# First block of a fused layernorm, state-space and mish kernel: one vector multiply placed behind the last rotation, the next x loaded two phases earlier, its layernorm pieces one to three first-layer tiles earlier

## The chip, the cores and the metric

The kernel runs on one core of one Trainium2 chip. The metric is device time in microseconds (us) of one execution, by default as the median of several. The profile's own span is about 2 us shorter than the device time of the same execution (623.9 against 626.0 for the kernel before), so spans are compared only with spans, and times with times.

Names used below: PE is the TensorE matmul engine, DVE is VectorE, ACT is ScalarE, POOL is GpSimd, SP is SyncE, which here only issues transfers. A bank is one of the eight pieces `ps[:, bank, :]` (512 fp32 values per partition) into which the kernel divides PSUM, the memory that its matmuls write to.

## The reference, cut to what matters

The input x is 2048 rows of 1024. After a layernorm the same rows feed two branches, which are added to x:

```python
xn = layernorm(x)
# branch A: complex diagonal recurrence over the 2048 rows
Bu = xn @ B_bar.T                      # 1024 complex states
h_t = Lam_bar * h_{t-1} + Bu_t
y  = 2 * real(h @ C.T) + xn * Dskip
# branch B: dense, mish, dense
h  = xn @ w1 + b1                      # 3584 wide
act = h * tanh(log1p(exp(h)))          # mish, written stably
out = x + y + act @ w2
```

The kernel works in four blocks of 512 rows. In each block PE does the first dense layer (28 tiles, f=0 to 27, eight matmuls each), the input projection of the recurrence (j=0 to 7, 16 matmuls each), then the second dense layer and the output projection, called the tail below.

## The kernel before: the parts that the change and the argument touch

The kernel issues each engine's work in the order of the source, and in its timelines each engine's operations run in that order. A helper works out the semaphore waits from the buffers that an operation reads and writes, so moving a line of source moves the operation in its engine's queue, and nothing else.

The end of the first layer and the side work of the first block (cut to block 0):

```python
def first_tile(blk, f):                 # PE: 8 matmuls into bank f % 8
    ...
    if fi == 1:
        item_done()                     # two tiles used up: SP may load the slot anew
    if f % GF == 0 and f >= 2 * GF:
        mish_mul(f // GF - 2)           # DVE: multiplies 0 and 1, at f = 14 and 21
    vop(... hb[:, hs, :] = ps[:, bank, :] + b1(f))       # DVE: frees the bank (L648)
    if f % GF == GF - 1:
        mish(f // GF)                   # ACT: exp, ln, tanh of seven tiles

def side(f):                            # block 0
    ...
    if f in (9, 11, 12, 13):  ln_skip(0, ...)
    if f in (14, 16, 18, 20): ln_stats_only(1, ...)      # statistics of the next x
    if f == 22:               ln_rsqrt()                 # 15 operations on 4 columns
    if f in (23, 24, 25, 26): ln_scale(1, ...)
    if f < 16 and f % 2 == 0: transpose_B(f // 2)        # SP: two transposing transfers
    if f >= 16:               transpose_C(f - 16)
```

POOL computes the phases of the rotation tables and issues the next x among them:

```python
for j in range(NJ):
    phases(j)                           # POOL: px, py, and the difference of both
    if j == 3:
        for q in range(NQ):
            load_x(PO, 1, q)            # four transfers of 256 KB
```

The input projection, with the rotation of its result on DVE (the "rotation" of j below means these four operations):

```python
def project_in(blk):
    for j in range(NJ):
        bank = 2 * ((j + 2) % 4)        # banks 4-5, 6-7, 0-1, 2-3, and again
        ... 16 matmuls into bank and bank + 1 (L661)
        for s in range(2):
            vop(... mt[:, s] = u * tab[:, s, j])          # L666, reads PSUM
        vop(... hT[:, 0, j] = mt[0, 0] + mt[1, 1])        # L669
        vop(... hT[:, 1, j] = mt[0, 1] - mt[1, 0])        # L671
        if j == (6 if blk == 0 else 4):
            mish_mul(2)                 # DVE, 128 x 3584 (L626)
        if j == 7 and blk:
            mish_mul(3)
```

The tail (L715) begins with 24 matmuls into banks 4 to 7; the next ones go to banks 0 to 3:

```python
for f in range(6):
    dense(f, ..., (4, 5, 6, 7))
for f in range(NF):
    dense(f, ..., (0, 1, 2, 3) if f < 6 else range(8))
```

## Time and profile before

Before the prediction the kernel had been timed three times: 625.97, 626.24 and 626.64 us.

| Kernel before | |
|---|---|
| median time | 626.24 us |
| span of the profiled execution | 623.9 us |
| PE busy / DVE busy / ACT busy | 99% / 75% / 40% |
| start of one 128x512 matmul to the next, undisturbed | 0.216 us |
| PE waits after its start-up | one, of 1.5 us |

The first line is the profile page's table of busy time per engine.

```profile
PE 616.7 (99%) x2961; PEld 287.4 (46%) x2961; DVE 466.0 (75%) x695; ACT 247.1 (40%) x162; POOL 50.0 (8%) x47
```

PE is the limit. The question for a small change is therefore only where PE stands still. The PE timeline of the kernel before (start, length, operation, count; a bracket tells the idle time just before the group and what ended it) shows one such place after the start-up:

```profile
83.80 3.62 PE L661 MATMUL ps<-xnT,BT 128*128 128x512 bf16 x16
87.25 5.78 PE L715 MATMUL ps<-ring,act 128*128 128x512 bf16 x26
94.55 5.79 PE L715 MATMUL ps<-ring,act 128*128 128x512 bf16 x26 [1.52 <-DVE mt L666]
```

The tail starts at 87.25 us, does its 24 matmuls and two more, and then waits. The bracket says 1.52 us, measured from the modelled end of the last matmul, which overlaps the next one when nothing waits. The real loss is counted from start to start: 26 matmuls at 0.216 us after 87.25 is 92.87 us, and the next one started at 94.55, so 1.68 us were lost.

The DVE timeline of the same stretch shows what was waited for:

```profile
67.45 2.34 DVE L666 TENSOR_TENSOR mt<-ps,tab 128x1024 bf16<-128x1024 f32 x2
...
87.14 2.36 DVE L666 TENSOR_TENSOR mt<-ps,tab 128x1024 bf16<-128x1024 f32 x2
...
90.21 2.02 DVE L626 TENSOR_TENSOR act<-act,hb 128x3584 bf16<-128x3584 bf16 x1
92.14 2.35 DVE L666 TENSOR_TENSOR mt<-ps,tab 128x1024 bf16<-128x1024 f32 x2
...
95.20 2.34 DVE L681 TENSOR_TENSOR_SCAN hT<-cs,hT 128x512 bf16<-128x512 f32 x2
```

The eight rotations start at 67.45 us and follow each other without a pause. The multiply of 1.93 us stands between j=6 and j=7. The products of j=7, which free banks 2 and 3, end at 92.14 + 2.35, so at 94.5 us, and PE starts then.

### The profile page before, as it was taken

The numbers are of one execution on the slowest core, as the hardware profiler recorded it, in microseconds if no ns is written. First come the engines' busy times: TensorE is split into PE (matmuls) and PEld (weight loads), VectorE is DVE, ScalarE is ACT, GpSimd is POOL, SyncE is SP. The second block draws the span as 40 slices with busy tenths as digits, with TensorE's granted clock in tenths as the row PEclk, the third lists the DMA queues.
The fourth block names the chain that finished last, engine by engine and source line by source line (L and its number), as shares of the span: only waits on it lengthen the run. The fifth ranks groups of instructions, "written<-read, shape, count | busy, mean of one in ns | idle before, by whom it ended". The sixth has DMA issues, their size and how long they took to land.

```text
span 623.9 us, 7415 instructions
## 1 busy us (share of the span) xinstructions
PE 616.7 (99%) x2961; PEld 287.4 (46%) x2961; DVE 466.0 (75%) x695; ACT 247.1 (40%) x162; POOL 50.0 (8%) x47
## 2 busy tenths in 40 slices
PE   8999999999999999999999999999999999999998
PEld 7644444444444444444444444444444444444443
DVE  6799999999457599999047759999624856999603
ACT  6679995441059950000008992000001999000000
POOL 1899000000100000000010000000000000000000
PEclk9999999999999999999999999999999999999999
DMA  9999976750365400764065520285204532033001
GB/s 268 215 259 249 258 152 172 200 166 3 106 198 169 134 2 7 232 171 132 13 190 144 159 101 1 77 227 153 85 35 134 167 137 68 1 131 106 1 0 68
DMA packets 124188, 79.41 MB, mean 127 GB/s; under 512 B 48890, under 2 KB 106490, under 8 KB 124154
## 3 DMA queue, kind: packets, MB, share of 16 engines
q1 hardware_dynamic: 120656, 71.58, 42.9%
q10 hardware_dynamic: 2538, 4.21, 1.8%
q0 software_dynamic: 960, 3.15, 1.8%
q8 instruction: 24, 0.39, 0.3%
q14 instruction: 10, 0.08, 0.0%
HBM read 63.19 MB, written 4.19 MB: 108 GB/s over the span
## 4 chain that ended last, share of the span: by engine, by line
PE 95%; DVE 3%; DMA 1%; issue 0%; SPq 0%; DVEq 0%
PE ps L715 48%; PE ps L641 29%; PE ps L661 16%; DVE mt L666 2%; PE ps L499 2%; DMA xx<-in_A_x_dram 1%; DVE hT L669 0%; PE ps L383 0%; DVE hT L671 0%; DVE xn L376 0%; SPq L287 0%; DVE xnT L392 0%; DVE xx L752 0%; DVE rs L371 0%; DVE stats L341 0%
## 5 line engine op out<-in xcount | busy, mean ns | idle before, releaser
L715 PE MATMUL ps<-ring,act 128*128 128x512 bf16 x896 | 194.2, 379 | 1.5 <-DVE mt L666 1.5
L641 PE MATMUL ps<-xnT,ring 128*128 128x512 bf16 x848 | 183.7, 379 | 0.0
L619 ACT ACTIVATE act<-hb 128x3584 bf16<-128x3584 bf16 x16 | 50.9, 3183 | 246.2 <-DVE hb L648 245.9
L715 PEld LDWEIGHTS ps<-ring,act 128*128 128x128 bf16 x896 | 87.5, 98 | 107.6 <-DVE mt L666 2.0
L641 PEld LDWEIGHTS ps<-xnT,ring 128*128 128x128 bf16 x848 | 82.9, 98 | 99.9
L648 DVE TENSOR_SCALAR hb<-ps,par 128x512 bf16<-128x512 f32 x112 | 82.8, 747 | 55.3 <-PE ps L641 54.0
L661 PE MATMUL ps<-xnT,BT 128*128 128x512 bf16 x512 | 111.2, 379 | 0.0
L715 PE MATMUL ps<-CT,hT 128*128 128x512 bf16 x512 | 111.2, 379 | 0.0
L666 DVE TENSOR_TENSOR mt<-ps,tab 128x1024 bf16<-128x1024 f32 x64 | 75.4, 1219 | 13.2 <-PE ps L661 11.7
L661 PEld LDWEIGHTS ps<-xnT,BT 128*128 128x128 bf16 x512 | 50.0, 98 | 60.5
L715 PEld LDWEIGHTS ps<-CT,hT 128*128 128x128 bf16 x512 | 50.0, 98 | 60.5
L752 DVE TENSOR_TENSOR xx<-ps,xx 128x1024 bf16<-128x1024 f32 (+1 forms) x17 | 19.5, 1161 | 72.0 <-PE ps L715 72.0
L681 DVE TENSOR_TENSOR_SCAN hT<-cs,qi,hT 128x512 bf16<-128x512 f32 x48 | 58.9, 1269 | 0.0
L621 ACT ACTIVATE act<-act 128x3584 bf16<-128x3584 bf16 x16 | 51.0, 3190 | 0.2
L620 ACT ACTIVATE act<-act 128x3584 bf16<-128x3584 bf16 x16 | 51.0, 3190 | 0.2
L686 DVE TENSOR_TENSOR mt<-hT,tab 128x1024 bf16<-128x1024 bf16 x64 | 41.4, 688 | 1.1
L626 DVE TENSOR_TENSOR act<-act,hb 128x3584 bf16<-128x3584 bf16 x16 | 32.3, 2017 | 1.3 <-ACT act L621 1.3
L287 POOL DMA_DIRECT2D xx<-in_A_x_dram x12 | 6.7, 559 | 254.8 <-DVE xx L752 250.5
L595 ACT ACTIVATE ct<-CT,cs 128x512 f32<-128x512 bf16 x16 | 11.5, 718 | 29.1 <-DVE CT L597 24.5
L620 ACT ACT_TABLE_LOAD x16 | 20.5, 1283 | 0.3
L621 ACT ACT_TABLE_LOAD x16 | 20.5, 1283 | 0.3
L681 DVE TENSOR_TENSOR_SCAN hT<-cs,hT 128x512 bf16<-128x512 f32 x16 | 18.7, 1208 | 0.0
(82 smaller groups left out, 280.2 us busy)
## 6 DMA issues: line engine op xcount, KB each, us to landing
ring<-in_B_w_dram SPq DMA_DIRECT2D x112, 512.0 KB, 3.7
out_dram<-xx ACTq DMA_DIRECT2D x15, 256.0 KB, 2.0
xx<-in_A_x_dram POOLq DMA_DIRECT2D x12, 256.0 KB, 4.0
xx<-in_A_x_dram SPq DMA_DIRECT2D x4, 256.0 KB, 3.4
dsk<-in_A_Dskip_dram SPq DMA_DIRECT2D x1, 256.0 KB, 6.4
out_dram<-xx ACTq DMA_DIRECT2D x2, 128.0 KB, 1.7
xnT<-xn SPq DMA_TRANSPOSE x12, 4.5
BT<-in_A_B_re_dram SPq DMA_TRANSPOSE x8, 5.9
```

The source lines that it names most:

```text
L619: aop(lambda e: e.activation(a, hs, AF.Exp), reads=[b_hb[g % 2]], writes=[b_act[g]])
L620: aop(lambda e: e.activation(a, a, AF.Ln, bias=1.0), reads=[b_act[g]], writes=[b_act[g]])
L621: aop(lambda e: e.activation(a, a, AF.Tanh), reads=[b_act[g]], writes=[b_act[g]])
L626: vop(lambda e: e.tensor_tensor(a, a, hs, op=ALU.mult), reads=[b_act[g], b_hb[g % 2]], writes=[b_act[g]])
L641: PE.mm(lambda e, k=k: e.matmul(ps[:, bank, :], lhsT=wt[:, k, fi * P:(fi + 1) * P], rhs=xnT[:, k, :], start=k == 0, stop=k == NK - 1), rea ...
L648: vop(lambda e: e.tensor_scalar(hb[:, hs, :], ps[:, bank, :], b1(f), None, op0=ALU.add), reads=[b_ps[bank], b_par], writes=[b_hbf[hs]])
L661: PE.mm(lambda e, j=j, ci=ci, k=k, bank=bank: e.matmul(ps[:, bank + ci, :], lhsT=BT[:, ci, j, k, :], rhs=xnT[:, k, :], start=k == 0, stop= ...
L666: vop(lambda e, s=s, u=u, j=j: e.tensor_tensor(mt[:, s, :, :], u, tab[:, s, j, :].unsqueeze(1).to_broadcast([P, 2, TB]), op=ALU.mult), rea ...
L681: vop(lambda e, ci=ci, init=init: e.tensor_tensor_scan(out=hT[:, ci, j, :], data0=cj("r", j).to_broadcast([P, TB]), data1=hT[:, ci, j, :], ...
L686: vop(lambda e, s=s: e.tensor_tensor(mt[:, s, :, :], hT[:, :, j, :], tab[:, s, j, :].unsqueeze(1).to_broadcast([P, 2, TB]), op=ALU.mult), ...
L715: PE.mm(lambda e: e.matmul(ps[:, u, :], lhsT=lhsT, rhs=rhs, start=st_, stop=last), reads=reads, writes=[b_ps[u]], first=st_, last=last)
L752: vop(lambda e: e.tensor_tensor(xr, src, xr, op=ALU.add), reads=b_src + [b_x], writes=[b_x])
```

## The change

The intent is to let j=7 free its banks before the multiply runs, and to spread the remaining DVE work of the first block so that the rotations start no later. The x of the second block has to arrive earlier for that. The whole diff:

```diff
     for j in range(NJ):
         phases(j)
-        if j == 3:
+        if j == 1:
             for q in range(NQ):
                 load_x(PO, 1, q)
@@ project_in
-            if j == (6 if blk == 0 else 4):
+            if j == 4 and blk:
                 mish_mul(2)
-            if j == 7 and blk:
-                mish_mul(3)
+            if j == 7:
+                mish_mul(3 if blk else 2)
@@ side(f), block 0
-            if f in (9, 11, 12, 13):
-                ln_skip(0, (9, 11, 12, 13).index(f))
-            if f in (14, 16, 18, 20):
-                ln_stats_only(1, (f - 14) // 2)
-            if f == 22:
+            if f in (9, 11, 12, 14):
+                ln_skip(0, (9, 11, 12, 14).index(f))
+            if f in (13, 15, 17, 18):
+                ln_stats_only(1, (13, 15, 17, 18).index(f))
+            if f == 19:
                 ln_rsqrt()
-            if f in (23, 24, 25, 26):
-                ln_scale(1, f - 23)
+            if f in (20, 22, 23, 24):
+                ln_scale(1, (20, 22, 23, 24).index(f))
```

No operation is added or removed. The order on PE, ACT and SP stays the same; DVE and POOL do the same operations in another order.

## The prediction

> **What bounds it.** TensorE. The page has PE busy 99% of a 623.9 us span; the chain of waits is 95% PE, 3% VectorE (DVE). Matmuls start every 0.216 us. After its start-up (about 10 us) PE stands still once: 1.5 us before the first block's second-layer matmuls (L715), released by DVE `mt` (L666). In the PE timeline the last matmul before it starts at 92.65 us, so the next could go at 92.87; it goes at 94.55. The loss is 1.68 us, 0.27%; nothing else on PE can be won.
>
> **Why that wait.** The tail opens with 24 matmuls on banks 4 to 7, then needs banks 2 and 3, which the last rotation (j=7) must read out. In the DVE timeline the eight rotations run back to back from 67.45 us at 3.28 us each, slightly faster than PE's 3.46 us per j. Between j=6 and j=7 stands the third mish multiply (L626, 90.21 to about 92.14, 1.93 us). So j=7's products end at 94.50, and PE goes.
>
> **Part 1, multiply after j=7.** j=7's products should end at 94.50 - 1.93 = 92.57, before 92.87: the wait disappears. The multiply lands before the recurrence; its result (tiles 14 to 20) is first read by PE near 111 us, some 15 us later. The recurrence starts when it did. The last coefficient matrix is ready at 155.3, PE needs it at about 161.5 (159.8 after the change): no new wait.
>
> **Part 2, x and layernorm earlier.** DVE has hardly any idle from 30 to 95 us; at the last eviction (f=27, 66.8 us) it runs 7 us behind PE (59.8). The order of the work changes, not its sum, so 67.45 hardly moves. Side effects: (a) POOL and DVE block each other: an `xx` sum took 1.64 us against 0.69 normally beside POOL's subtract (30.52 to 32.05), a 4-column multiply 1.25 against 0.16. The Trainium skill, "SBUF — State Buffer", section "Who interferes with whom", says that a DVE instruction with two SBUF inputs contends with a GpSimd instruction that reads SBUF; the trace agrees. The x issues (2.34 us of POOL) move from 37.4 to about 26.9 us, where DVE has slack, and push phases 2 and 3 later; collisions fall elsewhere. I estimate -1 to +0.5 us at the start of the rotations. (b) Reciprocal root and normalizations now precede more evictions: bank 5 (f=21) is freed at about 61 to 62 us (57.0 before), and PE wants it at 61.5 for j=0. A new PE wait of 0 to 0.7 us is possible. DMA is saturated until 78 us; x moves 1 MB forward, but weight tiles issued then have over 8 us of slack; stats need x at about 39 us.
>
> **Sum.** PE idle falls from 1.68 us to 0 to 0.5, best guess 0.2. 626.24 - 1.45 = **624.8 us**, range **624.2 to 626.0**. Chances: over 2% faster 0.01, within 2% 0.985, over 2% slower 0.005.
>
> **What shows it.** Right: PE's wait on `mt` before L715 is gone or below 0.3 us; the chain is PE alone from about 10 us on; the L626 multiply lies between the last rotation and the first scan; rotations start between 66.4 and 68; later blocks keep 152 us each. Wrong: a new PE wait on `hb` (L648) before L661 near 61 us; PE waiting for `ring` or BT near 27 to 45 us; DVE waiting for x near 39 us.
>
> **What would make it wrong.** Collisions with POOL delaying the rotations beyond 67.6 us, which brings the PE wait back one for one; the bank-5 wait; or x's transfer delaying a weight tile. None can cost more than about 2 us.

## The result, and the profile after

| | before | after |
|---|---|---|
| median of six runs, same rounds | 626.12 us | 624.57 us |
| lowest to highest | 625.74 to 626.64 | 624.34 to 625.61 |
| ratio, 95% interval | | 0.9977 (0.9965 to 0.9990) |
| span of the profiled execution | 623.9 us | 623.6 us |

Ratios here and below are the mean time of one kernel's fast runs over the mean of the other's fast runs of the same rounds, so they are not quite the ratio of the medians quoted. The change is 0.2% faster, and within the 2% that counts as the same.

The profiled execution of the changed kernel happens to be the slowest of its six (625.61 us, span 623.6; the other five have spans of 622.3 to 622.8). That made it more instructive. Its PE timeline:

```profile
53.49 3.63 PE L641 MATMUL ps<-xnT,ring 128*128 128x512 bf16 x15 [0.59 <-DMA ring<-in_B_w_dram]
57.62 3.63 PE L641 MATMUL ps<-xnT,ring 128*128 128x512 bf16 x16 [0.50 <-DMA ring<-in_B_w_dram]
61.08 27.79 PE L661 MATMUL ps<-xnT,BT 128*128 128x512 bf16 x125
88.71 23.47 PE L715 MATMUL ps<-ring,act 128*128 128x512 bf16 x106
```

The tail is one group with no bracket (88.71 us on): the wait on `mt` before the tail is gone. In its place PE waited twice for weight tiles (`ring`) before the last two pairs of first-layer tiles. The projection starts at 61.08 us. From the start of the dense matmuls at 21.74 us, 176 of them at 0.216 us would have brought PE there at 59.74, so 1.34 us were lost. That accounts for this execution: 1.68 us won, 1.34 us lost, and a span 0.3 us shorter.

The DVE timeline of the changed kernel, to set beside the one before:

```profile
66.60 2.35 DVE L666 TENSOR_TENSOR mt<-ps,tab 128x1024 bf16<-128x1024 f32 x2
...
89.57 2.35 DVE L666 TENSOR_TENSOR mt<-ps,tab 128x1024 bf16<-128x1024 f32 x2
...
92.64 2.02 DVE L626 TENSOR_TENSOR act<-act,hb 128x3584 bf16<-128x3584 bf16 x1
94.58 2.33 DVE L681 TENSOR_TENSOR_SCAN hT<-cs,hT 128x512 bf16<-128x512 f32 x2
```

The rotations start 0.85 us earlier, the multiply stands behind j=7, and the products of j=7 end at 91.92 us instead of 94.5. The scan starts 0.6 us earlier than before.

Where the late weight tile came from is read from SP's timeline of issues. The lines are one transfer issue each; the length is the time that SP's queue was held by it.

```profile
28.82 0.79 SPq L316 DMA_DIRECT2D ring<-in_B_w_dram  x1
29.65 7.40 SPq L606 DMA_TRANSPOSE BT<-in_A_B_re_dram  x1
37.09 3.03 SPq L606 DMA_TRANSPOSE BT<-in_A_B_im_dram  x1
40.22 0.53 SPq L316 DMA_DIRECT2D ring<-in_B_w_dram  x1
...
53.43 0.53 SPq L316 DMA_DIRECT2D ring<-in_B_w_dram  x1
```

Just after POOL issued x's four transfers (26.58 to 28.92 us), one transpose issue held SP's queue for 7.40 us. It is not that more bytes moved meanwhile: the profile's windows show 120 and 111 GB/s from 30 to 34 us, against 238 to 264 in the six microseconds before. What made the issue long is not shown. The weight loads stand behind transposes in the same queue. The load of tiles 26 and 27 went out at 53.43 us; PE wanted it before 57 us. In the kernel before, that load went out at 50.33:

```profile
45.05 3.47 SPq L606 DMA_TRANSPOSE BT<-in_A_B_re_dram  x1
48.57 1.66 SPq L606 DMA_TRANSPOSE BT<-in_A_B_im_dram  x1
50.33 0.53 SPq L316 DMA_DIRECT2D ring<-in_B_w_dram  x1
```

Three questions were left. Does the multiply alone carry the gain? Is the early layernorm of any use? And does the early x cause the waits for weights?

### The profile page after: what moved, and what is told of

The parts are those of the page before. It is cut to its first block, busy times and chain, and to the rows that moved or that the text cites. A ratio compares the mean times of both kernels' runs of the same rounds, so it can differ in the third digit from the quotient of the medians.

```text
span 623.6 us, 7360 instructions
## 1 busy us (share of the span) xinstructions
PE 613.7 (98%) x2905; PEld 287.2 (46%) x2961; DVE 465.0 (75%) x695; ACT 247.2 (40%) x162; POOL 49.4 (8%) x47
## 4 chain that ended last, share of the span: by engine, by line
PE 93%; ACT 2%; DVE 1%; issue 1%; DMA 1%; SPq 1%; ACTq 0%; DVEq 0%
PE ps L715 48%; PE ps L641 25%; PE ps L661 18%; PE ps L499 2%; DMA ring<-in_B_w_dram 1%; SPq L606 1%; ACT act L621 1%; ACT act L620 1%; ACT act L619 1%; DVE hb L648 0%; DVE act L626 0%; PE ps L383 0%; ACTq L294 0%; ACT L620 0%; ACT L465 0%
```

## The experiments

The theory at the start had two parts: the move of the multiply removes the 1.68 us wait by itself, and the wait for weights is an accident of the profiled execution. The rivals: the gain needs the earlier start of the rotations as well; or the early x always costs most of it. All runs gave correct results.

### The changed kernel again

No edit.

> The changed kernel once more. Theory (the multiply took 1.68 us of PE wait away; the two PE waits for weight tiles near 53 and 57 us in the profiled run were an accident of that run): span near 622.3, no PE wait for ring, ratio 0.9973 to 0.9980. Rival (the earlier x load always delays weight tiles by about 1.4 us and eats most of the gain): PE waits of 1 us or more for ring again, span near 623.6.

Measured: runs of 624.40 to 627.18 us, median 625.37; ratio 0.9988 (0.9977 to 1.0). The profiled execution (625.2 us span) was again the slowest of its group. PE waited for `ring` four times, 2.4 us in the list of waits; the last first-layer weight load went out at 54.32 us, behind a transpose issue of 6.29 us. Not all of that lateness can be x's: SP's load just before x was issued went out at 26.61 us, 2.0 us later than in the kernel before (24.58). Counted from start to start, PE lost 2.9 us (projection at 62.66 us, 59.76 without loss). One run, at a span of 622.3 us, was as fast as the theory said. So neither side holds as stated: the waits for weights are no single accident, and they do not come in every run.

### The multiply alone

```diff
-            if j == (6 if blk == 0 else 4):
+            if j == 4 and blk:
                 mish_mul(2)
-            if j == 7 and blk:
-                mish_mul(3)
+            if j == 7:
+                mish_mul(3 if blk else 2)
```

> Only the multiply after the last rotation; x and layernorm as before. Theory (the multiply alone carries the gain): rotations start at 67.45 as before, the products of j=7 end at 92.57 to 92.8, PE wait on mt below 0.2 us, no PE wait for ring, ratio 0.9973 to 0.9978, as good as the whole change or better. Rival (the earlier layernorm is needed too, because it starts the rotations 0.85 us earlier): a PE wait of 0.5 us or more is left, ratio 0.9985 or higher.

Measured: 624.10 to 624.95 us, median 624.30; ratio 0.9971 (0.9958 to 0.9983). The timelines of this kernel, first DVE:

```profile
67.41 2.34 DVE L666 TENSOR_TENSOR mt<-ps,tab 128x1024 bf16<-128x1024 f32 x2
...
90.38 2.36 DVE L666 TENSOR_TENSOR mt<-ps,tab 128x1024 bf16<-128x1024 f32 x2
...
93.45 2.02 DVE L626 TENSOR_TENSOR act<-act,hb 128x3584 bf16<-128x3584 bf16 x1
```

then PE:

```profile
56.49 3.63 PE L641 MATMUL ps<-xnT,ring 128*128 128x512 bf16 x16 [0.19 <-DMA ring<-in_B_w_dram]
59.95 27.79 PE L661 MATMUL ps<-xnT,BT 128*128 128x512 bf16 x125
87.58 24.77 PE L715 MATMUL ps<-ring,act 128*128 128x512 bf16 x112
```

The rotations start when they did before, the products of j=7 end at 92.74 us, and the tail runs through without a wait. The theory's number (0.9973 to 0.9978) was met or beaten, and the rival's remaining wait of 0.5 us is absent. The multiply alone carries the gain. The small wait for `ring`, 0.19 us, was not expected: x is loaded at the old time here.

### x and layernorm early, the multiply where it was

```diff
-            if j == 4 and blk:
+            if j == (6 if blk == 0 else 4):
                 mish_mul(2)
-            if j == 7:
-                mish_mul(3 if blk else 2)
+            if j == 7 and blk:
+                mish_mul(3)
```

(against the changed kernel)

> Only x and layernorm earlier; the multiply stays between j=6 and j=7. Theory: rotations start at 66.6 instead of 67.45, so the products of j=7 end at 93.7 and the PE wait on mt falls from 1.68 to about 0.8 us: ratio 0.9985 to 0.9990, or 1.000 where PE waits for ring. Rival (this part changes nothing): the wait stays at 1.5 us or more, ratio 1.000.

Measured: 625.54 to 629.44 us, median 626.11; ratio 1.0006 (0.9990 to 1.0022). The PE timeline:

```profile
59.92 27.99 PE L661 MATMUL ps<-xnT,BT 128*128 128x512 bf16 x125
87.75 5.78 PE L715 MATMUL ps<-ring,act 128*128 128x512 bf16 x26
94.12 18.09 PE L715 MATMUL ps<-ring,act 128*128 128x512 bf16 x81 [0.60 <-DVE mt L666]
```

The wait on `mt` fell from 1.52 to 0.60 us, but only half of that is a gain. The products of j=7 end at 94.07 us (93.7 expected), and the 27th matmul of the tail starts 0.43 us earlier than in the kernel before; the rest of the shorter wait is PE reaching the tail 0.50 us later (87.75 against 87.25). The span of 623.5 us, 0.4 less than the kernel before, agrees. The ratio over all runs shows no gain; one run of 629.44 us, which was not profiled and is unexplained, weighs on it. The projection takes 27.99 us where it takes 27.79 elsewhere. The list of waits names the cause:

```profile
PEld ps L661 <- DVE hb L648: 0.5, 1, 0.5
```

PE's weight load waited 0.5 us for an eviction of a first-layer tile, which is the wait for bank 5 that the prediction called possible; PE lost the difference of 0.2 us by it.

### The multiply moved and x early, the layernorm where it was

```diff
         phases(j)
-        if j == 3:
+        if j == 1:
             for q in range(NQ):
                 load_x(PO, 1, q)
```

(together with the edit of the multiply alone)

> The multiply moved and x loaded two phases up, layernorm pieces as before. Theory (the rotations' earlier start comes from moving x's four issues on POOL away from VectorE's two-input instructions, not from the layernorm order): rotations start at 66.3 to 66.9, no PE wait on mt. Rival (it comes from the layernorm order): they start at 67.3 to 67.6. The ratio is 0.9973 to 0.9980 under both, unless PE waits for ring, which x's time alone would then cause.

Measured: 624.34 to 625.75 us, median 624.93; ratio 0.9979 (0.9967 to 0.9991). The rotations start at 67.60 us, so the theory about POOL's issues is wrong and the rival right: moving x alone does not start them earlier. The profiled execution has no wait for `ring` at all, although x is early: its last first-layer weight load went out at 49.50 us. So early x does not by itself make the weights late.

The 0.85 us of the whole change come from early x and early layernorm together. Neither is enough alone, as a later run with early layernorm and late x shows (69.80 us). In the DVE timelines from 28.5 to 67 us, the time of every operation that took over 0.1 us longer than the shortest of its kind was summed: 4.4 us in the kernel before, 4.3 us with early x alone, and 3.6 to 3.7 us in the three profiles of the changed kernel. The difference of 0.7 us is of the size of the earlier start. It is a sum of several collisions that fall differently, so this is an account and not a proof.

### The whole change with the input-matrix transposes one pair later

```diff
-            if f < 16 and f % 2 == 0:
-                transpose_B(f // 2)
+            if f in (0, 4, 6, 8, 10, 12, 14, 16):
+                transpose_B((0, 4, 6, 8, 10, 12, 14, 16).index(f))
```

> The whole change, and the seven later pairs of input-matrix transposes issued one pair (two weight tiles) later on SyncE's queue, so that each weight load has one pair less before it. Theory (PE's waits for ring come from SyncE's in-order queue: transposes slowed by x's transfer hold the weight loads behind them): the last first-layer weight loads are issued 3 to 4 us earlier, no PE wait for ring above 0.2 us, all runs within 624.0 to 624.7, ratio 0.9968 to 0.9975. Rival (the transfers themselves share a full DMA, whatever the order): waits for ring of 1 us or more in the profile, runs up to 626 as before.

Measured: 624.28 to 625.59 us, median 624.52; ratio 0.9972 (0.9959 to 0.9984). There is no wait for `ring` in the profile, and the last first-layer weight load went out at 49.07 us. Five of six runs lie within 624.28 to 624.66; the sixth, at 625.59, misses the expectation, and it was not profiled. The wait of PE's weight load for bank 5 is there again (0.5 us, with the projection at 27.98 us). This fits the theory that order in SP's queue decides, but does not show it: two of the five profiles with the old order and early x had no wait either, and in this execution no transpose issue after the first pair took over 3.25 us. For the outlier it is open.

### The multiply alone with the same later transposes

The same edit on the kernel with only the multiply moved.

> Only the multiply moved, and the same later transposes. Theory: PE never waits for ring and waits under 0.1 us for mt: span 622.1 to 622.3, ratio 0.9967 to 0.9973, spread of runs under 0.5 us. Rival (multiply alone has no ring waits to lose): the same median as the multiply alone, within 0.1 us, and no smaller spread.

Measured: 624.16 to 625.25 us, median 624.67; ratio 0.9972 (0.9960 to 0.9985). The profiled execution has neither wait (span 622.3 us), although a transpose issue of 6.73 us stands at 41.85 us. The runs are no closer together than those of the multiply alone, so the expected smaller spread did not come. The edit is no gain on top of the multiply.

### x spread over four phases

```diff
-        if j == 1:
-            for q in range(NQ):
-                load_x(PO, 1, q)
+        if 1 <= j <= 4:
+            load_x(PO, 1, j - 1)
```

(against the changed kernel)

> The whole change, but x's four pieces are issued one each after phases 1 to 4 instead of all four after phase 1. Theory (x's burst of 1 MB stalls the transposes on SyncE): no transpose issue takes over 4 us, PE waits for ring below 0.5 us, ratio 0.9970 to 0.9980. Rival (the 1 MB costs SyncE's queue the same in sum, however it is spread): same waits for ring as the whole change, ratio 0.998 to 0.999.

Measured: 626.60 to 627.50 us, median 626.79; ratio 1.0008 (0.9995 to 1.0021). On SP's queue the theory was right: no transpose issue took more than 2.44 us, the last weight load went out at 48.22 us, and PE never waited for `ring`. But the kernel got slower than the changed one, by something that neither theory had named (the line numbers here are one lower):

```profile
60.14 1.89 PE L660 MATMUL ps<-xnT,BT 128*128 128x512 bf16 x8 [0.34 <-issue]
63.65 4.71 PE L660 MATMUL ps<-xnT,BT 128*128 128x512 bf16 x20 [1.62 <-DVE hb L647]
```

The first eight matmuls of j=0 (bank 4) run, and the second eight (bank 5) wait for the eviction of tile f=21. DVE did it at 62.84 us:

```profile
60.72 2.01 DVE L625 TENSOR_TENSOR act<-act,hb 128x3584 bf16<-128x3584 bf16 x1
62.84 1.41 DVE L647 TENSOR_SCALAR hb<-ps,par 128x512 bf16<-128x512 f32 x2
```

In the changed kernel the same eviction starts at 60.61 us, and in the kernel before at 56.30, because it has the reciprocal root behind this eviction. With the early layernorm order the reciprocal root and the second multiply both stand before the eviction of f=21, and there is no slack left: two microseconds of DVE delay are two microseconds of PE. The delay is most likely from other collisions with POOL: the sum of overlong DVE operations, counted as above, is 5.9 us here against 3.7 in the changed kernel, and DVE did not wait for x.

### The third multiply behind rotation 5

```diff
-            if j == (6 if blk == 0 else 4):
+            if j == (5 if blk == 0 else 4):
                 mish_mul(2)
```

> The kernel before, with the third multiply after rotation 5 instead of 6, so still ahead of the last rotation. Theory (only being behind the products of j=7 counts, since VectorE runs without a pause): j=7's products end at 94.5 as before, PE wait 1.5 us, ratio 0.9995 to 1.0005. Rival (it matters that it stood right before j=7): the wait falls by half or more, ratio 0.9987 or less.

Measured: the profiled execution ran for 1241.49 us, with matmuls 0.47 us apart; it is left out. The five runs are 625.82 to 627.11 us, ratio 1.0001 (0.9988 to 1.0015). That is the theory's number. For the timelines it was run once more:

> The kernel of the multiply after rotation 5 once more for a readable profile, since the first one was taken at half of TensorE's rate. Theory: products of j=7 end at 94.3 to 94.7 us, PE wait on mt 1.3 to 1.7 us. Rival: half of it or less.

Measured, one execution (626.66 us):

DVE:

```profile
68.26 2.34 DVE L666 TENSOR_TENSOR mt<-ps,tab 128x1024 bf16<-128x1024 f32 x2
...
87.73 2.02 DVE L626 TENSOR_TENSOR act<-act,hb 128x3584 bf16<-128x3584 bf16 x1
89.67 2.35 DVE L666 TENSOR_TENSOR mt<-ps,tab 128x1024 bf16<-128x1024 f32 x2
92.92 2.35 DVE L666 TENSOR_TENSOR mt<-ps,tab 128x1024 bf16<-128x1024 f32 x2
```

PE:

```profile
88.50 5.78 PE L715 MATMUL ps<-ring,act 128*128 128x512 bf16 x26
95.33 17.01 PE L715 MATMUL ps<-ring,act 128*128 128x512 bf16 x76 [1.06 <-DVE mt L666]
```

The products of j=7 end at 95.27 us, 0.6 us later than expected, because the rotations began at 68.26 instead of 67.45. From the first rotation to those products it is 27.01 us, against 27.04 in the kernel before and 25.32 in the changed one. So the place behind j=5 is no better than the place behind j=6, and only the place behind the products counts. PE's wait on `mt` was 1.06 us, less than expected, because in this execution PE had already lost time to a wait for `ring` of 0.9 us, and reached the tail later.

### The multiply alone and the whole change, once more side by side

> Only the multiply moved, again, beside the whole change on the same chip. Theory (the early x and layernorm cost time in some runs and bring none): median 624.2 to 624.6, slowest below 625.2, ratio 0.9970 to 0.9975. Rival (both versions are the same within noise): medians within 0.1 us of each other and equal spread.

> The whole change a third time. Theory: median 624.6 to 625.4, at least one run above 625.5, ratio 0.9977 to 0.9988, the profile with PE waits for ring or for hb before the first projection. Rival (its late runs belonged to two chips): no PE wait for ring, median as the multiply alone.

Measured on one chip: multiply alone 624.16 to 625.57 us, median 624.40, ratio 0.9972 (0.9959 to 0.9984); whole change 624.56 to 626.23 us, median 625.54, ratio 0.9983 (0.9969 to 0.9997). The multiply alone had two runs above 625.2, against the theory; the median of the whole change is 0.1 us above the range expected, and PE's wait for `ring` came as expected. The profile of one of them shows why:

```profile
57.57 3.63 PE L641 MATMUL ps<-xnT,ring 128*128 128x512 bf16 x16 [0.83 <-DMA ring<-in_B_w_dram]
```

So the wait for weights comes with late x, too, and early x can't be its only cause. The whole change's profile shows one of 0.97 us before the same tiles.

### The multiply moved and the layernorm early, x where it was

```diff
-        if j == 1:
+        if j == 3:
```

(against the changed kernel)

> Multiply moved and layernorm pieces early, but x loaded after phase 4 as before: the last corner of multiply, x, layernorm. Theory (early layernorm needs early x, and leaves bank 5 no margin: e7 lost 2 us of PE there when VectorE was 2 us later): VectorE waits for x at the first statistics (x landed at about 41 to 47 us, wanted at 39) or gets there later by collisions, bank 5 is freed at 63 to 65 us, PE waits 1 to 3 us for hb, ratio 1.000 to 1.003. Rival (the layernorm order alone is harmless): ratio 0.997 to 0.998.

Measured: 627.33 to 629.42 us, median 627.64; ratio 1.0025 (1.0011 to 1.0039), the slowest version of all, as the theory said. DVE waited 1.3 us for x at the first statistics, evicted f=21 at 63.82 us, and PE waited 1.05 us before j=0 and 1.62 us for bank 5. The early layernorm needs the early x.

### What the profiles together say of the waits for weights

Each row is one profiled execution. "Longest transpose" is of the input matrix (`BT`) and leaves out the first pair, which stands behind the start-up loads. The last column is the sum in PE's list of waits.

| kernel | x issued at | longest transpose issue | last first-layer weight load issued at | PE waited for ring |
|---|---|---|---|---|
| before | 37.4 us | 3.47 us | 50.33 us | 0 |
| whole change | 26.6 | 7.40 | 53.43 | 1.1 |
| whole change, again | 26.6 | 6.29 | 54.32 | 2.4 |
| whole change, third | 26.9 | 5.39 | 51.85 | 1.0 |
| x and layernorm early | 27.0 | 5.26 | 50.53 | 0 |
| multiply, x early | 27.0 | 5.06 | 49.50 | 0 |
| multiply alone | 37.3 | 5.21 | 51.35 | 0.2 |
| multiply alone, again | 37.8 | 4.96 | 51.94 | 0.8 |
| multiply behind j=5 | 37.5 | 6.75 | 52.80 | 0.9 |
| multiply, layernorm early | 37.6 | 4.18 | 51.14 | 0 |
| whole change, transposes later | 27.0 | 3.25 | 49.07 | 0 |
| multiply, transposes later | 37.5 | 6.73 | 50.33 | 0 |
| x spread | 26.7 to 44.8 | 2.44 | 48.22 | 0 |

PE waited in every execution in which that load went out at 51.35 us or later, and in none in which it went out at 51.14 or earlier. The kernel before stands about 1 us from that edge. With the transposes in their old order and x in one burst, PE waited in three of five executions with early x and in three of five with late x, and the last load went out at 49.50 to 54.32 us with early x and at 50.33 to 52.80 with late x. So the time of the burst is not shown to matter. The burst itself goes with a long transpose issue: in all twelve profiles with a burst, one of 3.25 to 7.40 us followed within 12 us, and in the one profile with x spread there was none above 2.44 us. One profile is little, and why a transpose issue gets longer is not shown.

Over all runs, eight of 17 of the whole change are above 625.3 us, and two of 11 of the multiply alone; the medians are 624.92 and 624.32 us. On each of the two chips where both ran, the multiply alone had the lower mean, by 1.07 and 0.75 us. The intervals of the ratios overlap, but the runs can be compared directly: if the two names are dealt out at random among the runs of each chip, a mean difference as large as the 0.91 us seen comes up in 0.6% of the deals. So on these 22 runs the multiply alone was faster than the whole change by about 0.15%, and it is simpler. Which part of the rest costs this is not shown.

## Why the prediction was right

The bound, the wait and its removal were right, and shown so by the experiments. One side step, the slack of the weight tiles, failed, and the closeness of the number is partly luck.

- **The limit and the wait.** Right. PE's only wait after the start-up was the one on the products of j=7. Every version with the multiply behind j=7 has no PE wait on `mt` before the tail; the two other versions profiled with the multiply ahead of it do (0.60 us in the early-only version, 1.06 us behind j=5).
- **Part 1, 1.68 us from the multiply.** Right, and shown alone. The multiply-only kernel ended its j=7 products at 92.74 us (92.57 predicted) and took 0.9971 and 0.9972 of the time, or about 1.8 us less.
- **Recurrence and tail afterwards.** Right. The scan started within 0.6 us of its old time, and the change brought no new wait later: a block still takes 152 us (first dense matmul at 164.68 us in the second block, and at 316.62 in the third).
- **Part 2a, rotations at 66.4 to 68 us.** Right in number: 66.60, 66.65 and 66.91 us in the three profiles. Half of the reason given, POOL's x issues out of DVE's way, was not enough: with early x alone they start at 67.60. The Trainium skill, "SBUF — State Buffer", section "Who interferes with whom", says that a DVE instruction with two SBUF inputs contends with a GpSimd instruction that reads SBUF. The trace before agrees for the `xx` sum of 1.64 us against 0.69, and the overlong DVE operations fell from 4.4 to 3.7 us in sum; which collision moved for which reason is not shown. And the earlier start has no value once the multiply is behind j=7.
- **Part 2b, bank 5.** Right as a possibility of 0 to 0.7 us: PE lost 0.2 us there in two profiles of related versions (`x` and layernorm early; transposes later), and 2.0 and 2.7 us, with the wait just before j=0, where DVE was two to three microseconds later. In the three profiles of the whole change itself there was no such wait, since the waits for `ring` had made PE late.
- **Weight tiles.** This step failed. The prediction said that tiles issued while x moves "have over 8 us of slack". The load issued then does: it went out at 28.82 us, for tiles that PE reached near 42.5. But that was not the margin that counts. SP made one issue after another, with gaps of at most 0.12 us until 55 us, so a long issue at 30 us also delays the loads behind it: the next one by 6.4 us (40.22 against 33.86 in the kernel before), and the last first-layer load still by 3.1 us, where the margin is about 1 us. PE lost 1.34 us by late loads in the profiled execution and 2.9 us in the second one, more than the "about 2 us" that the prediction allowed; and the waits came at 46 to 59 us, not at 27 to 45, where it said to look. It named "x's transfer delaying a weight tile" only among the things that could go wrong. That the earlier x is the cause is not shown, since kernels with late x waited too. The Trainium skill, "DMA: Bandwidth & Descriptors", section "Issuing engines are not separate DMA queues", says that transfers issued from any engine run on the same 16 DMA engines and interleave. The traces fit that: x from POOL's queue goes with a transpose issue on SP's queue of 3.25 to 7.40 us, where the median before the burst is 2.0 us. They do not show what the issue waited for.
- **The sum.** 624.8 us was predicted and 624.57 measured, with 1.45 us against 1.55. That it is so close is partly luck. The best guess held 0.2 us of PE idle; the three profiles of the whole change show about 1.0 to 2.9 us lost, all of it to `ring`, and the two repeats have medians of 625.37 and 625.54 us. The times spread to 627.18, outside the range.

## What to carry to other kernels

When one engine is the limit, look for its few real waits and move exactly the operation that stands in front of what it waits for; here moving one operation did at least as much as a three-part change. Work moved earlier for balance is not free: it stands before other operations with their own deadlines (a PSUM bank, a weight slot), so read the margin of those before moving it. A slack counted for a transfer is worth only as much as the margin of the last transfer behind it in the same in-order queue.

## What the Trainium skill lacked or had wrong

- "DMA: Bandwidth & Descriptors" has no figure for how long the issuing queue is held by a transposing transfer under load. Here it was 1.4 to 3.2 us (median 2.0) before x's burst, the first pair left out, and at the longest 3.25 to 7.40 us after a burst of four 256 KB transfers from POOL (twelve profiles). In the profiled execution of the changed kernel the next plain load in the queue was 6.4 us late. With the burst spread, in one profile, it stayed at 2.44 us or less.
- "SBUF — State Buffer", section "Who interferes with whom", calls the port pair that DVE and GpSimd share an exclusive lock, and says that a DVE instruction with two SBUF inputs contends with a GpSimd instruction that reads SBUF. The kernel before has a case in which no delay is seen: POOL's `py` operation, which reads SBUF, ran from 34.13 to 36.07 us, its usual 1.94 us, and DVE's two-input product (34.59 us, 0.69 us long) and sum (35.31 us, 0.69 us) inside it took their undisturbed times. The spans on POOL are rough, so this is an observation and not a rule.
- The same section gives no figure for what contention costs a tiny operation. A multiply on 4 columns took 1.25 us beside POOL's subtract instead of 0.16, and the whole 15-step reciprocal root lost about 1.8 us to three overlong operations.
- "TensorE: Matmul & The Clock Gate", section "Seeing it yourself", warns that the clock events of a trace can be unreliable. One execution here agrees: it ran at half rate (49 matmuls in 23.15 us, 1239.5 us in all) while the granted clock was recorded as 1.00 up to 800 us. No page says how often a single-core kernel meets this; here it was one execution, and its cause is open.
